# Two-layer decode attention and MLP with all gradients on one core: softmax by halves, joined layer norms, gelu by the logistic, and w1 turned in the softmax's gaps

## The chip, the core and the metric

The kernel runs on one core of one Trainium2 chip. Its time is the device time of one execution in microseconds (us). Before the change three runs gave 1210.46, 1213.57 and 1215.08 us; the median is 1213.57 us. A profile shows the engines by short names: PE is the matrix engine (PEld its weight loads), DVE the vector engine, ACT the activation engine, POOL the general engine; SP issues the loads from HBM, POOL the stores.

## What is computed

Two layers of one-token attention over a long cache, each followed by an MLP, and then the gradients of every input. Both layers use the same weights and the same cache. Batch is 2, the model width 1024, 32 query heads share 4 key/value heads of 128, the cache has 16384 positions, and the MLP is 3584 wide.

```python
def _layernorm(x, axis=-1, eps=1e-5):
    m = jnp.mean(x, axis=axis, keepdims=True)
    v = jnp.var(x, axis=axis, keepdims=True)
    return (x - m) / jnp.sqrt(v + eps)

def _A_ref(x, k_cache, v_cache, wq, wo):
    q = (x @ wq).reshape(B, Sq, Hq, Dh).transpose(0, 2, 1, 3)
    k = jnp.repeat(k_cache, rep, axis=1)
    v = jnp.repeat(v_cache, rep, axis=1)
    scores = jnp.einsum("bhqd,bhkd->bhqk", q, k) * (Dh ** -0.5)
    p = softmax(scores)
    o = jnp.einsum("bhqk,bhkd->bhqd", p, v)
    return o.transpose(0, 2, 1, 3).reshape(B, Sq, Hq * Dh) @ wo

def _B_ref(x, w1, b1, w2, b2):
    y = _layernorm(x)
    h = gelu(y @ w1 + b1)          # the tanh form
    return h @ w2 + b2

x = x + _A_ref(_layernorm(x), ...)
x = x + _B_ref(_layernorm(x), ...)
x = x + _A_ref(_layernorm(x), ...)
x = x + _B_ref(_layernorm(x), ...)
```

The outputs are the last x and the gradients of x, both caches, wq, wo, w1, b1, w2 and b2, in bfloat16. The MLP's input is normalised twice in a row, once outside and once inside `_B_ref`.

## The kernel before

**Data in time.** A group is one batch entry and one key/value head, so there are eight. Each group's K or V comes in four chunks of 1 MB (32 tiles of 128 positions). Weights come in chunks of up to 1 MB as well. Chunks live in slots: 14 in a fixed pool, and three to seven more in tiles that are unused at that time (`last`, half of `e1`, `ds1`). The class `Program` records the kernel as a list of pieces, and each piece names the chunks that it reads. `run` then walks the list, gives chunks to free slots in the order of first use, and issues each load on SP as soon as its slot's old content has had its last use. So SP loads in the order of first use, far ahead if slots are free, and waits if the next slot is still being read. The pieces are also the order of the instructions on every engine; nothing reorders them.

**Stages.** Forward attention of layer 0 (`attn_fwd(0, ...)`), MLP of layer 0, forward attention of layer 1, MLP of layer 1 forward and backward, backward attention of layer 1, MLP of layer 0 backward, backward attention of layer 0. The last stage also makes all weight and cache gradients (`kv_outputs`, `dw_units`) and stores them. Some chunks of K and V stay in their slots from the end of one stage to the start of the next (`keep0`, `keep1`).

**Forward attention.** It runs 128 steps, 16 to a group. A step turns eight K tiles on PE (L322, `ablock`), copies them out of PSUM on ACT or DVE, whichever a running balance favours (`copy_bf`, L191 and L194), and two steps later (`SKEW`) multiplies them by the queries (L636). Scores of a group fill two PSUM banks, one per half. `softmax` hangs its parts on later steps of the same count: `m0` and `m1` take maxima of the halves (L527, L532), `m2` turns them and joins them over partitions (L538 to L542), `m3` spreads the negative maximum (L547, L549), `ex` makes the exponentials, one ACT instruction for each head and half, with the maximum as a bias and the sum accumulated (L556), and `m4` adds the sums over partitions and inverts them (L566, L567). The product with V (L619) follows `LAG_F` = 24 steps behind the step that turned the matching K. Blocks of wq and wo for the next and the last head pair are spread between (L476, L495).

**Around the change.** `ln_fwd` and `ln_bwd` are generators; each `yield` marks where a sum over partitions by PE (`part_sum`, L379) is waited for, and `chain` emits other pieces at these places. `mlp_in` and `mlp_in_bwd` each run two of them in a row. `gelu_fwd` and `gelu_slope` work on tiles of 128 x 56. For layer 1 the rows of w1 are needed twice: as they are in `w1_fwd` (L656) and turned in `w1_bwd` (L693). `w1_turned` turns them (PE L349, copies L191, L194 or L352). The first two chunks are turned into two extra slots during the layer norms, the other six in place in `w1_fwd`'s loop. `wo_now` turns wo's blocks, eight pieces, between the gelu and `w1_bwd`. The backward attention's own first steps turn V tiles as the forward steps turn K.

## Time and profile before

| what | value |
|---|---|
| median of three runs | 1213.57 us |
| the profiled execution | 1217.15 us |
| its span, first to last instruction | 1215.4 us |
| mean granted PE clock | 0.841 of full speed |
| PE busy | 1049.3 us, 86% |
| DVE busy | 616.8 us, 51% |
| ACT busy | 585.2 us, 48% |
| read from HBM | 352.37 MB |
| written to HBM | 98.62 MB |

The profile is of one execution. Busy times count overlapped work on different engines separately. A wait is put down to the instruction that ended it. "Lnnn" is the line of the kernel before, as printed above, and names such as `kT<-tp` say which tile is written from which. The page divides the span into 40 slices; its digits are tenths busy:

```profile
PE   6888896688999888888889898988998899889996
...
DMA  9999999989999992999999885899999999999995
GB/s 343 379 420 421 421 421 421 368 320 357 401 419 422 418 379 103 376 420 421 418 404 351 304 345 197 310 405 362 409 418 363 378 411 420 378 397 406 416 414 203
```

Each slice is 30.4 us. DMA moves about 420 GB/s where it is full.

### The profile page before, as it was taken

Reading aid. Unit: us, or ns where it says so; the run is one execution under the profiler, and the core shown is the slowest. Engines: PE = TensorE matmul, PEld = TensorE weight load, DVE = VectorE, ACT = ScalarE, POOL = GpSimd, SP = SyncE. Lnnn points to the kernel's source line nnn. Section 1 sums busy time; section 2 is a strip of 40 time slices with the busy share of each in tenths; the row PEclk is TensorE's granted clock in tenths of the full one; section 3 lists DMA queues with packets and bytes.
Section 4 is the critical chain, followed back from the end, with each engine's and each line's share of the span. In section 5 each row is a group of like instructions: output and inputs, shape, how many; then the busy total and the mean of one; then the engine's idle time right before and its main releaser. Section 6 shows DMA issues by size and latency. Waiting matters only on the chain. (4 is left out here: it accounts for less than half of the span.)

```text
span 1215.4 us, 44602 instructions
## 1 busy us (share of the span) xinstructions
PE 1049.3 (86%) x19820; PEld 882.8 (73%) x19849; DVE 616.8 (51%) x1303; ACT 585.2 (48%) x1426; POOL 126.5 (10%) x216
## 2 busy tenths in 40 slices
PE   6888896688999888888889898988998899889996
PEld 5878896688899888888889887565565556556663
DVE  2333342234333424433333343877886787778775
ACT  1443343024433533233434332766775677667774
POOL 0000000000000000000000001322222222222222
PEclk8866675589666858789989987998998899999998
DMA  9999999989999992999999885899999999999995
GB/s 343 379 420 421 421 421 421 368 320 357 401 419 422 418 379 103 376 420 421 418 404 351 304 345 197 310 405 362 409 418 363 378 411 420 378 397 406 416 414 203
DMA packets 106045, 453.87 MB, mean 373 GB/s; under 512 B 8658, under 2 KB 8658, under 8 KB 75516
## 3 DMA queue, kind: packets, MB, share of 16 engines
q1 hardware_dynamic: 78780, 352.36, 73.7%
q0 software_dynamic: 27072, 98.66, 20.1%
q8 instruction: 155, 2.54, 0.8%
q14 instruction: 38, 0.31, 0.1%
HBM read 352.37 MB, written 98.62 MB: 371 GB/s over the span
## 5 line engine op out<-in xcount | busy, mean ns | idle before, releaser
L191 ACT COPY kT<-tp 128x512 int32<-128x512 int32 x377 | 220.7, 585 | 425.1 <-PE tp L322 351.3
L322 PE MATMUL tp<-ident,slot 128*128 128x128 bf16 x4224 | 374.4, 241 | 6.6 <-issue 3.9
L194 DVE COPY kT<-tp 128x1024 bf16<-128x1024 bf16 x259 | 178.9, 691 | 266.7 <-PE tp L322 218.3
L322 PEld LDWEIGHTS <-slot 128*128 128x128 bf16 x4224 | 289.9, 108 | 24.1 <-issue 10.0
L199 ACT CAST slot<-sc 128x512 bf16<-128x512 f32 x271 | 157.7, 589 | 51.3 <-PE sc L996 19.8
L202 DVE CAST slot<-sc 128x512 bf16<-128x512 f32 x227 | 154.4, 688 | 35.6 <-PE sc L996 16.1
L996 PE MATMUL sc<-last 128*128 128x512 bf16 x324 | 119.7, 388 | 17.2 <-ACT slot L199 5.3
L911 PEld LDWEIGHTS <-kT 128*128 128x128 bf16 x2048 | 80.7, 97 | 48.2 <-issue 31.1
L892 PEld LDWEIGHTS <-slot 128*128 128x128 bf16 x1856 | 79.0, 98 | 34.3 <-issue 10.3
L911 PE MATMUL sc<-qd,kT 128*128 128x8 bf16 x2048 | 90.6, 170 | 10.5 <-issue 10.4
L1003 POOL DMA_DIRECT2D out_dram<-slot x128 | 69.0, 539 | 280.4 <-ACT slot L199 174.8
L202 DVE CAST slot<-sb 128x512 bf16<-128x512 f32 x126 | 86.7, 688 | 18.3 <-PE sb L996 6.8
L636 PE MATMUL sc<-qd,kT 128*128 128x8 bf16 x2048 | 90.7, 172 | 0.9 <-issue 0.9
L199 ACT CAST slot<-sb 128x512 bf16<-128x512 f32 x128 | 75.4, 589 | 26.6 <-PE sb L1043 14.2
L556 ACT ACTIVATE e<-sc,negm 128x64 bf16<-128x64 f32 x256 | 75.9, 355 | 7.5 <-DVE negm L549 7.3
L636 PEld LDWEIGHTS <-kT 128*128 128x128 bf16 x2048 | 73.5, 100 | 0.2
L996 PE MATMUL sb<-last 128*128 128x512 bf16 x161 | 62.4, 387 | 6.6 <-ACT slot L199 1.6
L349 PE MATMUL tp<-ident,slot 128*128 128x128 bf16 x716 | 61.4, 244 | 5.8 <-DVE slot L194 2.0
L619 PE MATMUL sb<-e,slot 128*128 128x8 bf16 x1440 | 62.4, 176 | 3.5 <-DVE rbc L567 3.1
L556 ACT ACTIVATION_READ_ACCUMULATOR e<-sc,negm 128x1 f32 x256 | 63.6, 249 | 0.0
L1043 PE MATMUL sc<-last 128*128 128x512 bf16 x155 | 56.5, 384 | 4.6 <-DVE last L1031 3.4
L619 PEld LDWEIGHTS <-slot 128*128 128x128 bf16 x1440 | 56.8, 104 | 5.0 <-issue 3.8
(314 smaller groups left out, 1317.1 us busy)
## 6 DMA issues: line engine op xcount, KB each, us to landing
slot<-in_A_k_cache_dram SPq DMA_DIRECT2D x99, 1024.0 KB, 10.0
slot<-in_A_v_cache_dram SPq DMA_DIRECT2D x93, 1024.0 KB, 11.5
out_dram<-slot POOLq DMA_DIRECT2D x182, 512.0 KB, 10.6
slot<-in_A_wq_dram SPq DMA_DIRECT2D x30, 1024.0 KB, 9.8
slot<-in_A_wo_dram SPq DMA_DIRECT2D x22, 1024.0 KB, 11.8
slot<-in_B_w_dram SPq DMA_DIRECT2D x20, 896.0 KB, 13.7
last<-in_A_k_cache_dram SPq DMA_DIRECT2D x15, 1024.0 KB, 11.3
last<-in_A_v_cache_dram SPq DMA_DIRECT2D x11, 1024.0 KB, 16.0
```

Source lines behind the costliest of these rows:

```text
L191: S.copy(out=dst.bitcast(I32), in_=src.bitcast(I32))
L194: V.tensor_copy(out=dst, in_=src)
L199: S.copy(out=dst, in_=src)
L202: V.tensor_copy(out=dst, in_=src)
L322: PE.transpose(tp[:, j, :], t, ident[:])
L556: S.activation(out=e_of(l, g)[:, 8 * f:8 * f + 8, hh, :], in_=sc[f][:, hh, :].rearrange("p (a b) -> p a b", b=8), func=ACT.Exp, bias=h["ne ...
L619: PE.matmul(acc, lhsT=c.ap[:, ((vi % 4) * 8 + j) * 128:((vi % 4) * 8 + j + 1) * 128], rhs=e[:, vi, :, j], start=(vi == 0 and j == 0), stop ...
L636: PE.matmul(sc[t // 64][:, :, t % 64], lhsT=kT[:, j, :], rhs=qd[:, 0, g, l, :], start=True, stop=True)
L892: PE.matmul(sb[0][:, 0:8], lhsT=c.ap[:, ((vi % 4) * 8 + j) * 128:((vi % 4) * 8 + j + 1) * 128], rhs=d[:, vi, :, j], start=(vi == 0 and j = ...
L911: PE.matmul(scb[0][t // 64][:, :, t % 64], lhsT=kT[:, j, :], rhs=qd[:, 1, g, l, :], start=True, stop=True)
L996: PE.matmul(ps, lhsT=hold["blk"][:, 2 * (hc % 2) + u // 2, :], rhs=flat(qms[w][:, (u % 2) * 4:(u % 2) * 4 + 4, :]), start=True, stop=True)
L1003: GP.dma_start((dKv if w == 0 else dVv)[g, :, hc * 16:(hc + 1) * 16, :], stg.rearrange("p (t d) -> p t d", d=128))
```

## The change

Five things are changed together.

1. **Softmax.** The negative maximum is added to a whole half (128 x 512) in PSUM by DVE, and one ACT instruction takes the exponential of that half without bias or accumulation. The sum comes from the rounded exponentials: PE multiplies them by a matrix of ones into the first half's bank, DVE reduces the result over positions and inverts it. This is hung four steps later than the start of the product with V, and `LAG_F` is 22.
2. **Layer norms.** The two in a row become one, with variance term v(1 + eps) + eps squared, forward and backward.
3. **Gelu.** It is written as x times (1 - s), s the logistic value 1/(1 + exp(2cu)), and the slope uses s, 1 - s and a polynomial saved by the forward part. `gelu_out` writes h; for layer 1 it comes after the slope.
4. **w1 in layer 1.** Three chunks, not two, are turned into extra slots. Five of their twelve pieces stand in the last steps of forward attention, the other seven in the layer norm. At step 130 a piece without instructions names the four V chunks of the last group; in the order of loads they stand before w1's.
5. **First steps.** The first two turns of the next attention stage are made ahead, in the chain of `attn_in(1)`, and in those of `g3_` and `g1_`. Four of the eight pieces of `wo_now` move from before `w1_bwd` to that chain.

```diff
-LAG_F = 24
+LAG_F = 22
...
+    ones_all = const.tile([128, 128], BF16, name="ones_all")
+    V.memset(ones_all[:], 1.0)
...
+    def turns_ahead(c):
+
+        holds = [{} for _ in range(SKEW)]
+        pieces = [(turn_of(lambda i=i: [c.ap[:, (i * 8 + j) * 128:(i * 8 + j + 1) * 128] for j in range(8)], h), [c])
+                  for i, h in enumerate(holds)]
+        return pieces, (c, holds)
+
+    def ablock(tiles, use, uses, mids=(), hold=None):
...
+        if hold is None:
+            hold = {}
+            emit(turn_of(tiles, hold), uses)
...
-        V.tensor_scalar(out=vpe[:], in0=ps2, scalar1=1.0 / D, scalar2=LN_EPS, op0=ALU.mult, op1=ALU.add)
+        V.tensor_scalar(out=vpe[:], in0=ps2, scalar1=(1.0 + LN_EPS if twice else 1.0) / D,
+                        scalar2=LN_EPS * LN_EPS if twice else LN_EPS, op0=ALU.mult, op1=ALU.add)
...
+        if twice:
+            V.tensor_scalar(out=nm[:, 1, :], in0=nm[:, 1, :], scalar1=1.0 + LN_EPS, scalar2=None, op0=ALU.mult)
...
-            def ex(f, hs):
+            def less(f):
                 def fn():
-                    for hh in hs:
-                        S.activation(out=e_of(l, g)[:, 8 * f:8 * f + 8, hh, :],
-                                     in_=sc[f][:, hh, :].rearrange("p (a b) -> p a b", b=8),
-                                     func=ACT.Exp, bias=h["negm"][:, hh:hh + 1], scale=1.0,
-                                     accum_out=h["esum"][:, f, hh:hh + 1])
-                        load_of("act", 0.33)
+                    V.tensor_tensor(out=sc[f][:], in0=sc[f][:],
+                                    in1=h["negm"][:].unsqueeze(2).to_broadcast([128, 8, 64]), op=ALU.add)
+                    dve(0.7)
                 return fn
 
+            def ex(f):
+                def fn():
+                    S.activation(out=e_of(l, g)[:, 8 * f:8 * f + 8].rearrange("p a h b -> p h a b"),
+                                 in_=sc[f][:].rearrange("p h (a b) -> p h a b", b=8), func=ACT.Exp)
+                    load_of("act", 0.6)
+                return fn
+
             def m4():
-                pm3 = bank[:, 32:40]
+                ps = flat(sc[0][:])
+                e = of_group(Et[l], g)
                 for f in range(2):
-                    PE.matmul(pm3, lhsT=onesf[:], rhs=h["esum"][:, f, :], start=(f == 0), stop=(f == 1))
-                V.reciprocal(out=rbc[l][:, g, :], in_=pm3)
-                dve(0.2)
+                    PE.matmul(ps, lhsT=ones_all[:], rhs=e[:, f * 512:(f + 1) * 512], start=(f == 0), stop=(f == 1))
+                es = small.tile([128, 8], F32, name="esum")
+                V.tensor_reduce(out=es[:], in_=ps.rearrange("p (a h b) -> p h a b", h=8, b=8), axis=AX.XY, op=ALU.add)
+                V.reciprocal(out=rbc[l][:, g, :], in_=es[:])
+                dve(0.9)
...
-            at(base + 21, ex(0, range(0, 6)))
-            at(base + 22, ex(0, range(6, 8)))
-            at(base + 22, ex(1, range(0, 4)))
-            at(base + 23, ex(1, range(4, 8)))
-            at(base + LAG_F, m4)
+            at(base + 20, less(0))
+            at(base + 21, ex(0))
+            at(base + 21, less(1))
+            at(base + 22, ex(1))
+            at(base + 26, m4)
...
+                if s == 130:
+                    for c in range(4):
+                        vc[7, c] = chunk_v(order[7], c)
+                    emit(lambda: None, [vc[7, c] for c in range(4)])
+                for p in tail.get(s, ()):
+                    emit(*p)
...
+    def gelu_out(l):
+        hpre, q = saved[f"gelu{l}"][:2]
+        V.tensor_tensor(out=h_all[:, :, 2 * l:2 * l + 2], in0=q[:], in1=hpre[:], op=ALU.mult)
...
+        hpre, q, sg, pl = saved[f"gelu{l}"]
+        V.tensor_tensor(out=pl[:], in0=pl[:], in1=sg[:], op=ALU.mult)
+        V.tensor_scalar(out=pl[:], in0=pl[:], scalar1=1.0, scalar2=None, op0=ALU.add)
+        V.tensor_tensor(out=pl[:], in0=pl[:], in1=q[:], op=ALU.mult)
+        return pl
...
-        y1, r1 = yield from ln_fwd(xT[:], f"m{l}a")
-        y2, r2 = yield from ln_fwd(y1[:], f"m{l}b")
+        y, rstd = yield from ln_fwd(xT[:], f"m{l}", twice=True)
...
-        dn = yield from ln_bwd(dm[:], y2[:], r2[:], "dn")
-        dx = yield from ln_bwd(dn[:], y1[:], r1[:], "dx")
+        dx = yield from ln_bwd(dm[:], y[:], rstd[:], "dx", twice=True)
...
-    chain(lambda: mlp_in(0, xA0), 4)
+    chain(lambda: mlp_in(0, xA0), 2)
...
-    chain(lambda: attn_in(1, xM0), 2)
     aflush()
+    k_now, k_first = turns_ahead(chunk_k1(down[0], 0))
+    chain(lambda: attn_in(1, xM0), 2, k_now)
...
-    w1T = [P.chunk(), P.chunk()] + ws1[2:]
-    chain(lambda: mlp_in(1, xA1), 4, w1_turned(ws1, 0, w1T[0]) + w1_turned(ws1, 1, w1T[1]))
-    hps1 = w1_fwd(1, ws1, lambda j: w1_turned(ws1, j, w1T[j], act=False) if j >= 2 else ())
+    w1T = [P.chunk() for _ in range(3)] + ws1[3:]
+    w1_now = [p for j in range(3) for p in w1_turned(ws1, j, w1T[j], act=False)]
+    xA1 = attn_fwd(1, down, lambda: xM0, chunk_k1, chunk_v1, k_first, {130 + i: [w1_now[i]] for i in range(5)})
+    chain(lambda: mlp_in(1, xA1), 2, w1_now[5:])
+    hps1 = w1_fwd(1, ws1, lambda j: w1_turned(ws1, j, w1T[j], act=False) if j >= 3 else ())
...
-    for p in wo_now:
+    for p in wo_now[:4]:
         emit(*p)
...
-    chain(g3_, 2)
+    v_now, v_first = turns_ahead(chunk_v(up[0], 0))
+    chain(g3_, 1, wo_now[4:] + v_now)
...
-    chain(g1_, 2, wo_now)
+    v_now0, v_first0 = turns_ahead(chunk_v(down[0], 0))
+    chain(g1_, 1, wo_now + v_now0)
```

## The prediction, made before the changed kernel was run

> **What bounds the kernel now.** I began with the page's slices: the DMA row stands at 9 nearly everywhere, with dips at the changes of stage. Then I asked for busy time by stage (columns: stretch, length, busy time and instructions of PE, PEld, DVE, ACT, POOL, then granted clock, DMA share, GB/s):

> ```profile
> 0.00:200.00 200.00, 164.28 (x3457) 159.10 (x3457) 64.98 (x151) 73.17 (x291) 3.03 (x11) 0.72 1.00 403
> 200.00:234.00 34.00, 17.73 (x471) 16.48 (x471) 5.49 (x31) 5.08 (x33) 1.41 (x2) 0.50 0.95 376
> ...
> 270.00:436.00 166.00, 151.66 (x3286) 148.31 (x3284) 61.35 (x129) 70.99 (x289) 0.00 (x0) 0.72 1.00 400
> 436.00:487.00 51.00, 41.41 (x828) 39.07 (x825) 16.96 (x59) 19.30 (x60) 1.38 (x2) 0.70 0.54 206
> ...
> 500.00:645.00 145.00, 128.12 (x3028) 125.48 (x3029) 56.75 (x132) 57.39 (x99) 0.00 (x0) 0.90 1.02 415
> ...
> 762.00:1190.00 428.00, 387.07 (x5310) 250.16 (x5336) 332.19 (x575) 298.38 (x549) 109.91 (x188) 0.97 1.00 393
> ```

> The rows are forward attention of layer 0; its tail, layer norms and w1 product; forward attention of layer 1; its tail, MLP and w1's backward; backward attention of layer 1; backward attention of layer 0 with the outputs. The reader should see that the DMA engines are full (1.00 to 1.02) in the four long rows and half empty (0.54) in the fourth shown, for 51 us. Who holds them there stands in the waits of the DMA queue over that stretch:

> ```profile
> SPq L286 <- PE sb L693: 25.5, 1, 25.5
> ```

> The next K/V load sat 25.5 us until `w1_bwd` (L693) gave back a buffer. So whatever lets PE reach L693 sooner is gained, if later stages follow. To see whether PE or DMA leads before it, I set issues against uses. The first w1 load of layer 1 is issued at 412.91 and lands 18.2 us later (its row in the DMA view), at 431.1; PE first reads it at 450.93 (rows: start, length, engine, line, what, count):

> ```profile
> 412.91 8.67 SPq L291 DMA_DIRECT2D slot<-in_B_w_dram  x2
> ```

> and PE's rows around it:

> ```profile
> 436.24 0.36 PE L636 MATMUL sc<-qd,kT 128*128 128x8 bf16 x8
> ...
> 445.19 3.56 PE L619 MATMUL sb<-e,slot 128*128 128x8 bf16 x128 [0.30 <-DVE rbc L567]
> ...
> 450.93 1.87 PE L349 MATMUL tp<-ident,slot 128*128 128x128 bf16 x16
> ...
> 459.67 2.34 PE L656 MATMUL sc<-m_all,slot 128*128 128x2 bf16 x84 [1.55 <-DVE sc L652]
> ...
> 486.25 0.85 PE L693 MATMUL sb<-dh_all,last 128*128 128x2 bf16 x28
> ```

> A lead of 20 us, while in layer 0's forward stage PE waits on loads (L476 on wq 6.2 us, L495 on wo 4.7). So layer 0's forward stage is bound by DMA, and from the first w2 product on by PE. PE's own waits in layer 1's forward stage are three, nearly all softmax (who waited: total, times, longest), and one group's look like this:

> ```profile
> PE sb L566 <- ACT e L556: 9.0, 6, 2.0
> PE sb L619 <- DVE rbc L567: 2.3, 7, 0.5
> PE sb L538 <- DVE mx L533: 1.6, 2, 0.8
> ```

> ```profile
> 402.59 0.34 PE L566 MATMUL sb<-esum,onesf 128*128 128x8 f32 x2
> 404.36 0.39 PE L566 MATMUL sb<-esum,onesf 128*128 128x8 f32 x2 [1.44 <-ACT e L556]
> 405.05 0.36 PE L619 MATMUL sb<-e,slot 128*128 128x8 bf16 x8 [0.30 <-DVE rbc L567]
> ```

> The sums over partitions (L566) wait for 16 exps, then PV waits for the reciprocal. Last, the clock: the stage's mean of 0.72 is 44% at full and 56% at half speed, some 93 us at half:

> ```profile
> 381.66:398.72 17.06, 17.06 (x353) 16.95 (x349) 4.82 (x10) 4.10 (x7) 0.00 (x0) 0.50 1.02 418
> ...
> 408.96:419.20 10.24, 9.44 (x257) 9.13 (x254) 4.19 (x9) 3.63 (x7) 0.00 (x0) 1.00 1.01 420
> ```

> Without any idle time PE still stayed at half speed for 17 us; a plain step (L619, L636, L322) is 1.28 us there and 0.86 us at full.

> **The change, part by part.** Sums are against the profiled execution: 1217.15 us, its span 1215.40 and 1.75 around it. It lies 3.58 above the median, 1213.57, so I carry the difference over.

> *Layer 0's forward stage.* Eight softmaxes get shorter, worth nothing: DMA at 1.00 for 200 us hides them. Without that cover they would be worth what layer 1's are. Between 200 and 234 the DMA idles 0.05 x 34 = 1.7 us because w1 buffers come back late; the joined layer norm (one round less, 215.40 to 218.98 = 3.6 us) and the shorter exps remove that cause, but no more than 1.7 can be had, since PE then waits for loads (1.6 us for w2 at 234.12). In `attn_in(1)` two of three K transposes move under the layer norm: 2.88 us at 267.71 become one step of 0.61 to 1.01, gain 1.9. Together 3.6 (bounds 1.9 and 5).

> *Softmax in layer 1, eight groups.* Removed: PE waits 9.0 + 2.3 = 11.3 us. ACT loses 16 pairs of L556 per group,

> ```profile
> L556 ACT ACTIVATE e<-sc,negm 128x64 bf16<-128x64 f32 x256 | 75.9, 355 | 7.5 <-DVE negm L549 7.3
> ...
> L556 ACT ACTIVATION_READ_ACCUMULATOR e<-sc,negm 128x1 f32 x256 | 63.6, 249 | 0.0
> ```

> 4.5 us from first to last (439.41 to 443.95), and gains two exps of 128x512, by the nearest row (L199, a PSUM cast of that shape, 589 ns) 1.2 us. DVE gains two subtractions at 0.68 (L837, same shape, from PSUM; writing back to PSUM is shown nowhere) and a reduction at 0.69 (L527): 2.1 us per group, under 61 of 166 us busy. PE exchanges two float32 products (L566, two passes each, 0.34 + 0.39 in the fence) for two 128x512 ones (L996, 388 ns each): even, and four steps after PV has begun. New wait: PV's first block needs negation 0.17, subtraction 0.68, exp 0.59, some 0.1 between each: 1.7 us after L547, with two steps (1.71 at full clock) before it. Queued behind it on PE are this step's transposes, hence the kT copies. Bounds per group 0 and 1.2 (a DVE copy of 0.69 in front and 0.5 of ACT backlog); I take 0.3, near zero since two steps cover it: 2.4 in all. So 11.3 - 2.4 = 8.9, bounds 1.7 and 11.3.

> *The clock* may add to this: with the 1.8 us holes gone some half-speed time may go, from 0 to 93 x (1 - 0.86/1.28) = 30 us. I take 1, because a cap follows at once: in the tail PE now reads w1's first chunk when the last scores are done (L636, 436.24 + 0.36 = 436.6). That load moves ahead of two wo loads (2.5 us each at 420 GB/s) and, with the 3.6 from above, lands at 431.1 - 5.0 - 3.6 = 422.5. PE can't pass it by more than 436.6 - 422.5 = 14.1. Hence 3.6 + 8.9 + 1 = 13.5 there. SP's order changes only there and by LAG_F, which asks for each V chunk two steps sooner, no load more; POOL loses two pow operations (0.7 each) and no store is passed.

> [...]

> *From 436.6 to the first L693 after 486.25: 50.4 us.* (a) Scores to PV, 8.6 us until 445.19: the chain until the negation ends takes 2.8 (439.38), subtraction, exp and gaps 1.4, so 4.2; PE meanwhile has the rest of PV (0.9), two small products (1.0) and 36 of w1's transposes (16 took 1.87 at half speed: 4.2). I take 7.0, gain 1.6. (b) Sums as wide products, at most 0.5 lost. (c) Layer norm, 8.6 us (451.06 to 459.67): one round less, but PE must do 48 transposes in it, 5.6, plus two sums 0.9, ends 2.0: 8.5, gain 0.1. (d) w1's third chunk is turned by then and leaves `w1_fwd`'s loop: 461.87 to 464.97, gain 3.1. (e) gelu and slope: 18 DVE operations (481.01 to 485.50) become 13 of about 0.2, plus a reciprocal's extra 0.3 and an exp: 3.8; before, eight wo pieces on ACT (1.07 per two) held PE for 5.2. Gain 1.4. Sum 5.7. 84 transposes at 117 or 66 ns (16 in 1.05 at full) are 4.3 us apart; I take half, 2.1. So 7.8, bounds 4 and 12.

> At L693 the gain is 13.5 + 7.8 = 21.3. The DMA queue's supply before it ended about 467 (share 0.43 from 465 to 470); moved by 3.6 it ends at 463.4, and L693 comes at 487.2 - 21.3 = 465.9, so the hole shrinks from 20 to 2.5 us and DMA keeps up.

> *The g3 and g1 chains.* One yield instead of two, but all fills now stand before the one sum. g3: 32 wo and 16 V transposes, then one half round (494.86 to 496.96): zero, bounds 1 either way, since the four moved wo pieces and the two skipped steps cancel. g1: 739.35 to 749.98, 10.6, plus two turns of 1.0 before; after, 80 transposes 8.4, sum 0.4, half round 2.1: 10.9 against 12.6, less 0.6 if a third of the unexplained 1.83 us of issue (742.63) recurs: gain 1.1; plus 0.6 from gelu's slope. 1.7, bounds 0 and 4. Layer 0's backward stage is untouched and DMA is empty before it (share 0.01 from 750 to 761.5), so it starts earlier by what PE gained.

> Sum: 21.3 + 0 + 1.7 = 23.0. 1217.15 - 23.0 = 1194.15; on the median, 1213.57 - 23.0 = 1190.6.

> **The rivals.** *The waits only change places* (0.17): subtraction and exp delay PV as much as the exps did; for it, PV's wait is on the same chain and DVE carries it too; against, 1.3 us replaces 4.5. Then 3.6 + 5.7 + 1.7 = 11: 1202.6. *The clock wakes up too* (0.15): for it, full-speed stretches end at an exp wait; against, the 17 us row. The cap binds at 14.1, B gets its 12, the chains 4: 30, so 1183.5. *Nothing to see* (0.04): the gain is given back in the last stage, DMA-full for 428 us; against, PE there has 90% and loads wait for it: 1212. *Slower* (0.08): writing PSUM in place, and exp with a strided output, cost triple, 2.0 and 1.8 us; it decides from there on. The chain becomes 4.2 against 1.7, wait 2.5, and 5 more on DVE and ACT delays the kT copies by 2, so 4.5 for 1.4 removed: 8 x 3.1 = 25 lost, against 3.6 + 5.7 + 1.7 kept: +14, 1227. Against it: L840, a DVE product of that shape with strided operands, takes 691 ns.

> **How the numbers follow.** Main case 0.56, 1185 to 1197, at 1190.6. A difference under 0.5%, 6.1 us, can't be told from none: faster is below 1207.5. Faster 0.56 + 0.17 + 0.15 = 0.88, same 0.04, slower 0.08. The range 1180 to 1205 takes in the main case, both faster rivals and the bounds.

> **What would show it.** Right: exps near 0.6 and subtractions near 0.7 us; PE's waits for ACT in layer 1's forward stage from 9 to 2; the queue's wait for `w1_bwd` from 25.5 to under 8; the stretch from the last scores to `w1_bwd` near 43. Wrong: PE waiting on w1 in the tail by more than 2 us, PV waiting over 1 us per group, or a last stage longer than before.

## The result, and the profile after

The changed kernel takes 1209.86 us (median of 20 runs, 1200.55 to 1214.3) beside 1215.59 us for the kernel before (20 runs taken with them): a ratio of 0.9949, 95% interval 0.993 to 0.9967. That is a gain of about 6 us where 23 were predicted, and the time lies above the predicted range of 1180 to 1205. The profiled execution has a span of 1209.6 us. The same kernel measured again, on another chip, gave 1206.69 us and 0.994 (0.9911 to 0.9969), with a profiled span of 1204.6 us.

To see where the gain arose and where it went, I cut the three profiles at the same products on PE: the first and last score product of layer 1's forward attention (L636 before, L661 after), the first product of `w1_bwd` in layer 1 (L693, L724), and the first and last score product of each backward attention (L911, L937). All numbers are us; the last two columns are for the two profiles of the changed kernel.

| stretch | before | after | again | gain predicted | gain measured |
|---|---|---|---|---|---|
| start to first score product of layer 1 | 270.4 | 271.1 | 270.6 | 3.6 | -0.7, -0.2 |
| its forward attention, to the last score product | 166.0 | 158.4 | 157.4 | 9.9 | 7.6, 8.6 |
| to the first product of `w1_bwd` | 49.8 | 41.9 | 42.0 | 7.8 | 7.9, 7.8 |
| `w1_bwd` and g3's chain | 16.5 | 18.9 | 19.1 | 0 | -2.4, -2.6 |
| backward attention of layer 1 | 196.4 | 199.1 | 194.8 | 0 | -2.7, 1.6 |
| MLP backward of layer 0, g1's chain | 61.7 | 62.9 | 63.3 | 1.7 | -1.2, -1.6 |
| last stage to the end | 454.6 | 457.3 | 457.4 | 0 | -2.7, -2.8 |
| span | 1215.4 | 1209.6 | 1204.6 | 23.0 | 5.8, 10.8 |

The changed kernel's busy time over four of these stretches (columns as in the prediction's first view):

```profile
271.10:429.50 158.40, 144.31 (x3293) 138.35 (x3298) 57.66 (x126) 58.83 (x103) 0.00 (x0) 0.79 1.01 403
429.50:471.40 41.90, 35.99 (x729) 33.35 (x727) 15.91 (x50) 13.40 (x26) 0.69 (x1) 0.71 0.81 315
490.30:689.40 199.10, 176.11 (x4193) 172.25 (x4191) 76.00 (x172) 79.14 (x136) 0.00 (x0) 0.90 0.97 377
752.30:1171.70 419.40, 376.51 (x5147) 243.04 (x5172) 322.72 (x559) 290.06 (x534) 107.23 (x183) 0.97 0.98 386
```

In the first row the clock rose (0.72 before, 0.79 now); in the second the DMA engines' hole shrank (share 0.54 before, 0.81 now). The queue's longest wait for `w1_bwd`, in the waits of the DMA queue from 440 to 480, fell from 25.5 to 18.9 us:

```profile
SPq L288 <- PE sb L724: 20.5, 7, 18.9
```

The softmax's own instructions came out as costed. In the groups by line (busy, mean ns, idle before) the subtraction in PSUM takes 694 ns and the exponential of a half, with its strided output, 608:

```profile
L573 DVE TENSOR_TENSOR sc<-sc,negm 128x512 f32<-128x512 f32 x32 | 20.8, 694 | 0.5
L580 ACT ACTIVATE e<-sc 128x512 bf16<-128x512 f32 x32 | 19.2, 608 | 5.0 <-DVE sc L573 4.9
```

What is new stands in PE's waits over layer 1's forward attention. Before, the list was 9.0 us for the exps, 2.3 for the reciprocal, 1.6 for the maximum. Now it begins so:

```profile
PE tp L321 <- issue: 4.5, 3, 1.7
PE sb L644 <- issue: 2.7, 2, 1.5
PE sb L494 <- issue: 2.5, 2, 1.8
PE sb L644 <- ACT e L580: 1.6, 4, 0.6
```

The waits for the exps are down to 1.6 us, but PE now idles for "issue", that is for nothing which the profile can name. With short gaps counted it is 11.0 us in the stage, where the kernel before has 1.3. The timeline shows what such a stall looks like; it falls into the middle of eight transposes whose tiles and banks are all there:

```profile
300.24 0.27 PE L321 MATMUL tp<-ident,slot 128*128 128x128 bf16 x2
302.25 0.51 PE L321 MATMUL tp<-ident,slot 128*128 128x128 bf16 x6 [1.75 <-issue]
```

Where the stalls fall tells the cause. Counted in PE's matrix products, the eight longest of the stage end at numbers 5335, 5718, 5974, 6484, 6612, 6995, 7378 and 7506; every distance is a multiple of 127 to 128. Each product has its weight load, so that is 256 instructions. The page's list of DMA queues (packets, MB, share) has a queue that moves code:

```profile
q8 instruction: 154, 2.52, 0.8%
```

It moved 154 packets of 16 KB, and PE ran 39567 instructions (19762 products, 19805 weight loads): 257 for each packet. In the trace's packet records the packet at 299.89 to 300.96 comes just before the stall's end at 302.25. In layer 1's forward attention, where the DMA engines are full (share 1.01 after, 1.00 before), two of these packets are never much less than 6 us apart: the median distance is 6.12 us after and 6.22 before, the shortest 5.86 and 5.78. The trace of before shows distances of 3.3 to 4.7 elsewhere, where the engines' share was 0.96 or less; the trace of after has a single one of 4.1 us at a share of 1.0, in the backward stage, so full engines don't hold up every packet. Counted from the stalls, no packet of the two traces starts more than 1.1 times 256 instructions ahead of the code that it brings, not even in the last stage, where the packets are 10.2 us apart (median): in these traces PE never had much more than one piece in store.

So I formed theory F, an inference from these records: in this stage PE can't run faster than its code arrives, 256 instructions in 6.1 us. The stage has 2 x 3296 instructions, 25.75 pieces, 157 us. From 166 us the softmax could win 9, whatever waits it removed. The rivals: the stalls are PE's own (P); the share of half clock sets the stage (K, and C in one expectation); the full DMA engines set it directly (D); any lead is lost in later stages (G).

### The profile page after: what moved, and what is told of

It reads as the page before. It is cut to its first block, busy times and chain, and to the rows that moved or that the text cites. A ratio compares the mean times of both kernels' runs of the same rounds, so it can differ in the third digit from the quotient of the medians.

```text
span 1209.6 us, 44046 instructions
## 1 busy us (share of the span) xinstructions
PE 1036.5 (86%) x19762; PEld 864.8 (71%) x19805; DVE 605.5 (50%) x1266; ACT 555.2 (46%) x996; POOL 125.1 (10%) x214
## 5 line engine op out<-in xcount | busy, mean ns | idle before, releaser
L191 ACT COPY kT<-tp 128x512 int32<-128x512 int32 x427 | 250.4, 586 | 428.1 <-PE tp L321 399.9
L321 PE MATMUL tp<-ident,slot 128*128 128x128 bf16 x4224 | 368.6, 238 | 12.6 <-issue 7.1
L321 PEld LDWEIGHTS <-slot 128*128 128x128 bf16 x4224 | 284.2, 107 | 29.8 <-issue 12.8
L194 DVE COPY kT<-tp 128x1024 bf16<-128x1024 bf16 x209 | 144.5, 691 | 302.7 <-PE tp L321 257.0
L199 ACT CAST slot<-sc 128x512 bf16<-128x512 f32 x271 | 157.8, 589 | 51.7 <-PE sc L1022 18.9
L918 PEld LDWEIGHTS <-slot 128*128 128x128 bf16 x1888 | 80.5, 98 | 43.1 <-issue 18.8
L937 PEld LDWEIGHTS <-kT 128*128 128x128 bf16 x2048 | 80.8, 97 | 37.7 <-issue 20.5
L661 PE MATMUL sc<-qd,kT 128*128 128x8 bf16 x2048 | 90.7, 171 | 3.6 <-issue 3.5
L937 PE MATMUL sc<-qd,kT 128*128 128x8 bf16 x2048 | 89.9, 170 | 1.0 <-issue 0.8
L199 ACT CAST slot<-sb 128x512 bf16<-128x512 f32 x128 | 75.4, 589 | 28.6 <-PE sb L1069 16.0
L661 PEld LDWEIGHTS <-kT 128*128 128x128 bf16 x2048 | 73.2, 99 | 4.1 <-issue 3.9
L362 PE MATMUL tp<-ident,slot 128*128 128x128 bf16 x692 | 58.6, 239 | 6.9 <-issue 2.9
L644 PE MATMUL sb<-e,slot 128*128 128x8 bf16 x1280 | 56.7, 176 | 8.3 <-ACT e L580 3.5
L644 PEld LDWEIGHTS <-slot 128*128 128x128 bf16 x1280 | 50.2, 102 | 11.9 <-issue 7.6
L362 PEld LDWEIGHTS <-slot 128*128 128x128 bf16 x692 | 48.3, 108 | 12.4 <-issue 9.8
L191 ACT COPY slot<-tp 128x512 int32<-128x512 int32 (+1 forms) x52 | 29.8, 574 | 52.5 <-PE tp L362 52.1
## 6 DMA issues: line engine op xcount, KB each, us to landing
slot<-in_A_k_cache_dram SPq DMA_DIRECT2D x101, 1024.0 KB, 10.1
out_dram<-slot POOLq DMA_DIRECT2D x182, 512.0 KB, 10.5
```

Source lines behind the costliest of these rows:

```text
L191: S.copy(out=dst.bitcast(I32), in_=src.bitcast(I32))
L194: V.tensor_copy(out=dst, in_=src)
L199: S.copy(out=dst, in_=src)
L321: PE.transpose(tp[:, j, :], t, ident[:])
L362: PE.transpose(tp[:, j, :], t, ident[:])
L644: PE.matmul(acc, lhsT=c.ap[:, ((vi % 4) * 8 + j) * 128:((vi % 4) * 8 + j + 1) * 128], rhs=e[:, vi, :, j], start=(vi == 0 and j == 0), stop ...
```

## The experiments

Each kernel is told by its edit. In the first four expectations the forward stage is counted from the first use of wq, some 5 to 7 us earlier than in the table; what is measured is given by the table's marks.

### Fewer bytes in layer 1's K and V loads, before and after

```diff
+    few = [32]
     def ld_kv(src, g, c):
+        n = few[0]
         return P.chunk(lambda ap: nc.sync.dma_start(
-            ap.rearrange("p (t d) -> p t d", d=128), src[g, :, c * 32:(c + 1) * 32, :]))
+            ap[:, 0:n * 128].rearrange("p (t d) -> p t d", d=128), src[g, :, c * 32:c * 32 + n, :]))
...
+    few[0] = 8
     xA1 = attn_fwd(1, ...)
...
     attn_bwd(1, ...)
+    few[0] = 32
```

> The kernel before, with the K and V loads of layer 1's two attention stages cut to a quarter of their bytes (the last three quarters of each of these chunks keep what an earlier load left there, so layer 1's scores and sums are of other data; the instructions are the same). Theory F: PE's stalls with no releaser ('issue') come when its next 256 instructions are not loaded yet; a 16 KB piece of code arrives every 6.0 us at best while the DMA engines are full and every 3.3 to 4 us while they are not. Then in backward attention of layer 1 'issue' falls from 17.2 us to under 4 and the stage from 201 to about 186; in forward attention of layer 1, where the kernel before has only 1.3 us of it, the stage stays within 3 us of 171.6, since its waits for the exps (9.1) remain. Rival P: the stalls are PE's own or come with its instruction mix; then 17.2 and 201 stay within 2 us. Rival M (the matrix products wait for loads in a way that the records don't name): both stages shrink, forward by as much as backward in share.

> The changed kernel with the same cut (layer 1's K and V loads at a quarter of their bytes, the rest of each chunk left as an earlier load left it). Theory F: the softmax's removed waits came back as waits for code, so without full DMA engines the forward attention of layer 1 loses its 11.0 us of 'issue' (to under 3) and goes from 164.9 to about 155, so that beside the kernel before with the same cut the softmax is worth 13 to 17 us in that stage instead of 6.7; backward attention of layer 1 goes from 204 to about 187. Rival P: 11.0, 164.9 and 204 stay within 2 us. Rival C (the stage is set by the share of half clock): 'issue' may go, but the stage stays within 3 us of 164.9 unless the mean clock rises above 0.80.

Measured: 1194.15 us for the kernel before with the cut, 1161.4 for the changed one (one run each; 1215.32 is the median of before there). The two attention stages of layer 1, first of the kernel before with the cut, then of the changed one with it:

```profile
266.40:432.90 166.50, 149.66 (x3298) 146.08 (x3296) 61.67 (x130) 70.64 (x288) 0.00 (x0) 0.74 0.52 179
497.10:675.10 178.00, 166.44 (x4193) 163.72 (x4191) 76.73 (x173) 78.45 (x135) 0.00 (x0) 0.96 0.57 194
```

```profile
269.00:404.40 135.40, 128.89 (x3303) 123.95 (x3300) 57.45 (x126) 58.45 (x103) 0.00 (x0) 0.93 0.64 218
461.60:642.00 180.40, 169.89 (x4190) 167.22 (x4189) 76.23 (x172) 78.97 (x136) 0.00 (x0) 0.93 0.55 191
```

With the engines half empty (shares 0.52 and 0.64) the forward stage of the kernel before stays at 166.5 us, but that of the changed kernel falls from 158.4 to 135.4, and its "issue" from 11.0 to 2.0. The backward stage falls by 18 us in both, its "issue" from 17 to 5.5, where under 4 was expected. In neither full-load stage did PE wait for a load, so the loads' own lateness doesn't explain this (against M). P, stalls that are PE's own, falls. F's sizes were too small: 10 us were expected in the forward stage and 23 came, because the clock rose as well, from 0.79 to 0.93. Of 127 steps, 113 ran wholly at full clock (74 before the cut), in 1.02 us each instead of 1.15. The main reading, from one profile of each kernel: the softmax is worth 31 us in this stage with the engines half empty, where code packets come as close as 3.7 us, and 7.6 with full ones, where the shortest distance is 5.9. Of the 31, 20.8 are PE's busy time (149.7 to 128.9 at the higher clock), the rest waits.

### The softmax alone, and all but the softmax

Edits: the kernel before with the functions `less`, `ex`, `m4` and their places, `ones_all` and `LAG_F` = 22 of the change; and the changed kernel with those of before and `LAG_F` = 24.

> The kernel before with the new softmax alone (whole halves, subtraction in PSUM, sums as wide products, a lag of 22 steps), nothing else of the change. Theory F: forward attention of layer 1 is as in the changed kernel, 165 (+-3) with about 10 us of 'issue' and under 3 us of waits for ACT, and the stretch from the last scores to the first use of w1_bwd about 49; the time is 1206 to 1211, that is nearly all that the whole change gives. The prediction's sum: 8.9 in the stage plus 1.6 in the tail, so 1205 (on 1215.6), with no new 'issue'. Rival G (what the front gains is given back in the last stage): 1214 or more.

> The changed kernel with the old softmax (16 exps per group, sums of exps, a lag of 24 steps), everything else of the change kept. Theory F: forward attention of layer 1 is back at 171 (+-3) with under 3 us of 'issue'; the stretch to the first use of w1_bwd stays near 44 (8.1 shorter came from the joined layer norm, gelu and w1's early turns, about 1.6 of it from the softmax), 2 to 3 us of that are lost again in the chain after w1_bwd, whose four pieces of wo now stand before its sum; the time is 1210 to 1214. The prediction's sum: 23.0 less 10.5 for the softmax, 12.5 gained, so 1203. Rival G: 1214 or more.

Measured: 1206.64 us for the softmax alone, ratio 0.9936 (0.9912 to 0.996), and 1212.55 us for all the rest, 0.9983 (0.9959 to 1.0006). The softmax alone gives 8.7 us where the prediction's sum has 10.5, and can't be told apart from the whole change; the rest gives 2.8 where the sum has 12.5, and can't be told from no change. With the softmax alone the forward stage takes 159.1 us with 9.5 of "issue" and 2.0 of waits for ACT; without it 167.6 with 0.6 and 12.3. From the last score product to `w1_bwd` it is 47.7 us with the softmax alone and 45.5 with the rest alone, 2.1 and 4.3 less than before: both parts gain there. Behind it the rest loses 2.8 us in g3's chain (19.3 beside 16.5) and 1.9 in g1's (63.6 beside 61.7). Rival G isn't general, since the softmax's 7 us reach the end.

### Shorter rows in the K and V loads

Edit, on the softmax alone: 16 (then 8) consecutive positions per partition instead of 128, in loads and stores alike.

```diff
-    Kv = A_k_cache.rearrange("b h (p t) d -> (b h) p t d", p=128)
+    Kv = A_k_cache.rearrange("b h (a p t) d -> (b h) p a (t d)", p=128, t=16)
...
-            ap.rearrange("p (t d) -> p t d", d=128), src[g, :, c * 32:(c + 1) * 32, :]))
+            ap.rearrange("p (a x) -> p a x", x=2048), src[g, :, c * 2:(c + 1) * 2, :]))
```

> The kernel before with the new softmax alone (1206.6 us), and another order of the tokens in the K and V chunks: 16 consecutive tokens per partition instead of 128, so that a load's rows are 4 KB long instead of 8 KB and a store of dK or dV is one piece of 512 KB with the same 4 KB rows. Theory S (size): a 16 KB piece of PE's code waits behind packets of loads that a DMA engine has taken up, and an 8 KB packet took 0.32 us; with 4 KB packets pieces come every 5 us or less while the engines are full, 'issue' in the two attention stages of layer 1 falls from 9.5 and 15.8 us to under 6 and 10, and the time to 1190 to 1200. Rival N (only fullness counts): pieces still come every 6.0 to 6.3 us, 'issue' stays within 3 us, the time within 3 us of 1206.6. Rival L: smaller rows cost the DMA engines rate, layer 0's forward stage (bound by DMA) gets longer than 199 by 4 us or more and the time is above 1210.

> The same with 8 consecutive tokens per partition: rows of 2 KB in loads of K and V and in stores of dK and dV. Theory S: pieces of code come every 4 to 5 us, 'issue' falls to under 3 and 6 us, the forward attention of layer 1 from 159 to 145 to 150 if loads keep up, the time to 1180 to 1195. Rival N: as for 4 KB, within 3 us of 1206.6 but for the stores. Rival L: above 1212, the last stage (417 us from its first to its last score product) longer by 5 us or more because its stores have 2 KB rows.

Measured: 1215.49 us (0.997 to 1.0039 of before) and 1235.85 us (1.0121 to 1.0209). S falls: code came every 6.26 us in both (median in the forward stage), so the time of a piece doesn't hang on the size of the packets around it, and "issue" rose from 9.5 to 14.8 and 12.7 us. N had this right and the times wrong. L holds: layer 0's forward attention, which DMA bounds (share 1.00 in the profile of before), went from 184.4 us to 188.3 and 196.3 between its score products. Here rows should stay long.

### Pieces of wo before `w1_bwd`, code moved, the sum first

Three kernels around the chains. The first puts all eight pieces of wo back before `w1_bwd` (`for p in wo_now`, and `chain(g3_, 1, v_now)`). The second adds 64 transposes of the identity at the start of the changed kernel. The third is the first with a new order in `chain`:

```diff
         for i in range(gaps):
-            n = -(-len(fill) // (gaps - i))
-            for f in fill[:n]:
+            for f in fill[:gaps]:
                 emit(*f)
-            fill = fill[n:]
+            fill = fill[gaps:]
             emit(lambda: next(hold["g"], None))
+        for f in fill:
+            emit(*f)
```

> The changed kernel with all eight pieces of wo before w1_bwd, as in the kernel before (the change moved four of them behind it, into the wait for the sum). Theory F: the pieces took 4.8 us between w1_bwd and the sum (two of them 1.46 us late for code) where the chain waits for nothing, so without them the stretch from the end of w1_bwd to the first product of backward attention falls from 13.1 to 9 us while w1_bwd starts 2.3 us later; net 1 to 2.5 us, 1207.5 to 1209. Rival (the prediction's zero): the two cancel and the time stays within 1 us of 1209.9. Rival G (any lead is lost in the stages that follow): 1209 to 1211, with the lead of 2 us at the first product of backward attention gone at its last.

> The changed kernel with 64 transposes of the identity more on PE in its first microseconds (128 instructions, half a piece of code), so that every later piece of code ends half a piece earlier in the work; nothing else. Theory A (place): the last 3 us that the changed kernel loses against the softmax alone come from where its pieces of code happen to end (1.5 us between w1_bwd and the sum, 2.3 us around the last w1_bwd); the stalls then sit elsewhere, the stage from first to last product of backward attention of layer 1 moves by 2 to 5 us from 199 and the time by 2 to 5 us from 1209.9, either way. Rival B: the time stays within 1.5 us of 1209.9 and the stages within 1 us; the place of the pieces doesn't matter, only their number.

> The changed kernel with all eight pieces of wo before w1_bwd (as in the run before, 1205.7 us) and with the transposes that fill a layer norm's wait placed behind its last sum where they stood ahead of it: one piece ahead of the sum of a norm with one round, two ahead of each sum of a norm with two, all others behind the last. The data for the sum are there 0.7 us after the last product, while 64 to 80 transposes ahead of it held it until 4.1 us (g3) and 7.7 us (g1) after; behind the sum they run under the half round of 2.2 us in which PE waited. Theory F: from the end of w1_bwd to the first product of backward attention 8.1 us becomes 6.2, in layer 0 from 20.5 to 18.3, and in layer 1's mlp_in 10.1 becomes 8.8; 5 us in all, of which stages paced by code keep most: 1200 to 1203. Rival G (a lead is lost in the stages that follow): 1204.5 or more. Rival Z (the transposes' copies on DVE delay the chain by what the order saves): the three stretches stay within 0.5 us and the time within 1.5 us of 1205.7.

> The changed kernel once more, on the chip of the run before, as its measure and for a second look at its stages: forward attention of layer 1 from first to last score product within 1.5 us of 158.4, the stretch to w1_bwd within 1 us of 41.9, backward attention of layer 1 within 3 us of 199.1, the last stage's score products within 3 us of 419.4; time 1207 to 1212.

Measured: 1205.69 us (0.9901 to 0.9953 of before) for the first, 1207.68 (0.9915 to 0.9974) for the second, 1204.03 (0.9898 to 0.9952) for the third, and 1206.69 for the changed kernel again, on the third's chip. The first was faster than the 1207.5 to 1209 expected, the third slower than its 1200 to 1203, and the changed kernel's second backward stage of layer 1, 194.8 us, lies outside the 3 us around 199.1.

What the chain lost is plain in PE's timeline of the changed kernel after the last product of `w1_bwd` (start, length, engine, line, what, count, idle before):

```profile
477.25 1.33 PE L362 MATMUL tp<-ident,slot 128*128 128x128 bf16 x11
480.04 2.42 PE L362 MATMUL tp<-ident,slot 128*128 128x128 bf16 x21 [1.46 <-issue]
482.28 1.89 PE L321 MATMUL tp<-ident,slot 128*128 128x128 bf16 x16
483.96 0.53 PE L392 MATMUL sc<-lb_s,onesf 128*128 128x4 f32 x2
486.54 0.34 PE L804 MATMUL sb<-gA_all,ds 128*128 128x2 bf16 x8 [2.05 <-DVE gA_all L780]
```

The sum (L392) needs data that DVE had finished 0.7 us after the last product, and stands behind 48 transposes until 483.96; then PE idles 2.05 us with nothing left to fill. The same place with the sum first:

```profile
481.57 1.01 PE L321 MATMUL tp<-ident,slot 128*128 128x128 bf16 x8
482.39 0.59 PE L392 MATMUL sc<-lb_s,onesf 128*128 128x4 f32 x2
482.84 1.01 PE L321 MATMUL tp<-ident,slot 128*128 128x128 bf16 x8
484.96 0.35 PE L805 MATMUL sb<-gA_all,ds 128*128 128x2 bf16 x8 [1.11 <-DVE gA_all L781]
```

From the end of `w1_bwd` to the first product of backward attention it takes 13.1 us in the changed kernel, 8.1 with wo before and 7.4 with the sum first as well; g1's stretch goes from 20.9 to 18.8 and layer 1's layer norm from 10.1 to 9.3, each within 1.2 us of what was expected (Z falls). The totals follow less clearly: 1204.0 against 1206.7 on one chip, with runs of the changed kernel from 1198 to 1214, so a gain of 2 to 3 us is likely and not shown. Moving the code by half a piece (128 instructions) shifted the backward stage by 3.3 us against the first profile, but the changed kernel's own two profiles differ there by 4.3, so neither this nor the total says anything about the place of the pieces.

The stall itself does. Both profiles of the changed kernel have it after the 11th of the 32 transposes, that is after 235 products from the start of `w1_bwd`. With the code moved by half a piece it is gone from there:

```profile
477.83 3.58 PE L362 MATMUL tp<-ident,slot 128*128 128x128 bf16 x32
```

With wo before, the 32 transposes stand ahead of `w1_bwd`, and the stall comes after 203 of its 224 products, again 235 from the same point of the code (the rows of its last 28):

```profile
477.72 0.33 PE L724 MATMUL sb<-dh_all,ds 128*128 128x2 bf16 x7
479.45 0.72 PE L724 MATMUL sb<-dh_all,ds 128*128 128x2 bf16 x21 [1.41 <-issue]
```

So it sits at a place in the code and not at a place in the work, as F has it. Without it the stretch of `w1_bwd` and g3's chain takes 17.1 us instead of 18.9 and 19.1.

### Half the products, and wide products

Two cuts in the product with V, each in both kernels. First, every second tile of V is left out and the others get 128 columns; then all eight products get 128 columns.

```diff
+                    if l == 1:
+                        e2 = of_group(Et[l], vg)[:, vi // 2 * 128:vi // 2 * 128 + 128]
+                        for j in range(0, 8, 2):
+                            PE.matmul(sb[vpos % 2][:, 272:400], lhsT=..., rhs=e2, ...)
+                        return
...
-                        for j in range(0, 8, 2):
+                        for j in range(8):
```

> The changed kernel with the product of e and V in layer 1's forward attention done for every second tile of V only (four of each step's eight products left out, so layer 1's attention output is of half of V), and the other four with 128 columns of e instead of 8: a pair of weight load and product with 128 columns takes 76 ns on PE (8 in 0.61 us) and one with 8 columns 45 ns (8 in 0.36), so four of the one take 0.31 and eight of the other 0.36 us: almost the same time on PE with 1024 instructions, four pieces of code, less in the stage; all loads are as they were. Theory F: the stage loses four times 6.1 us: from 157.4 to 158.4 (two looks) to 133 to 140, or up to 148 if loads come late first, and its 'issue' falls from 11 to 12 us to under 5. Rival P (PE's own work or its clock sets the stage): 154 to 159. Rival D (the DMA engines, full in this stage, set it): 154 to 159 with new waits for DMA in place of 'issue'.

> The same cut in the kernel before (every second tile of V left out in layer 1's forward attention, the others with 128 columns). Theory F: there the waits for the exps set the stage and code came in time (1.3 us of 'issue'), so the stage stays within 6 us of 166. Rival P: it gets shorter by as much as the changed kernel's. If both shrink alike, the number of PE's instructions counts by PE's own time and not by the code's arrival.

Measured: the stage takes 144.2 us in the changed kernel, its "issue" 4.0 us, and 153.0 in the kernel before. The first fits F, with loads late at last: 6.4 us of waits for DMA in the stage, and then PE stands before w1 (waits from 269 to 430):

```profile
PE tp L362 <- DMA slot<-in_B_w_dram: 11.3, 1, 11.3
```

w1's first chunk was usable at 425.4, so that is the other cap on a lead there (the prediction put it at 422.5). The second run is a miss for F: within 6 us of 166 was expected, and it fell by 13, with the clock at 0.91 instead of 0.72. The cut had moved instructions and clock at once and told nothing apart. Hence two more runs, with the count kept:

> The changed kernel with all eight products of e and V per step in layer 1's forward attention, each with 128 columns of e instead of 8 (so layer 1's attention output holds other sums; nothing is left out). The instructions are as many as before, loads too; a pair of 128 columns takes 76 ns where one of 8 takes 45, so PE has 0.25 us more to do per step at full clock, 32 us in the stage. Theory F: 51 instructions of PE per step at 6.1 us for 256 make 1.22 us, 156 us in the stage, whatever PE does in a step as long as it does it in less; at full clock a step would be 0.86 + 0.25 = 1.11, so the stage stays between 156 and 162 if the wider products keep the clock as high as in the two runs with four of them (0.91 to 0.96). Rival P (PE's work sets the stage): 157.4 plus most of 32, 175 or more. Rival K (the stage's length is the share of half clock): with a mean clock above 0.9 the stage falls below 150.

> The same in the kernel before. Theory F: the code's pace is the same floor of 156 us, the exps' waits (9 to 12 us) come on top as far as the code hasn't caught up in them: 160 to 170, though PE has 32 us more to do than in the 166 us of before. Rival P: 185 or more. Rival K: below 155.

The forward stage of the changed kernel with wide products, then of the kernel before with them:

```profile
268.60:425.40 156.80, 150.50 (x3296) 145.36 (x3301) 57.89 (x126) 59.04 (x103) 0.00 (x0) 0.99 1.01 404
```

```profile
267.90:433.20 165.30, 152.65 (x3300) 149.36 (x3298) 62.10 (x130) 70.62 (x288) 0.00 (x0) 0.97 0.98 396
```

PE had some 32 us more to do at full clock, and the clock was 0.99 instead of 0.79, yet the stage takes 156.8 us beside 158.4 and 157.4. The kernel before with them takes 165.3, within the 160 to 170 expected. Neither PE's work alone (P, 175 or more) nor its clock alone (K, below 150) sets it, and the DMA engines don't either (D), for with the same loads it took 144.2. It is 25.75 pieces at 6.1 us, 157.

One rival is left by these two runs: more work at a higher clock could come out the same by chance, for PE was busy 150.5 of the 156.8 us. The other kernels exclude it. The softmax alone with rows of 4 KB has the same products, 8 columns wide, and its forward stage reads

```profile
277.60:434.50 156.90, 138.63 (x3294) 132.10 (x3299) 57.87 (x126) 58.76 (x103) 0.00 (x0) 0.86 1.02 395
```

From this kernel to the one with wide products PE's busy time goes from 138.6 to 150.5 us, the clock from 0.86 to 0.99 and "issue" from 14.8 to 3.6, and the stage stays at 156.9 and 156.8. All eight profiles of kernels with the new softmax, all their products, full loads and rows of 4 or 8 KB lie between 156.8 and 160.0. This settles F for the forward stage. The backward stage of layer 1 has 2 x 4192 instructions, 32.75 pieces, 200 us by the same count, and takes 193 to 200 in the kernels with full loads and rows of 4 or 8 KB; some of its packets are closer together, so the count is only an upper mark there.

## Why the prediction was wrong

**Where the missing gain lies.** The sum was 23.0 and the first profile shows 5.8. Of the 17.2 us between them 4.3 lie before layer 1's first score product, 2.3 in its forward attention, 2.4 in g3's chain, 2.7 in layer 1's backward attention, 2.9 in g1's stretch and 2.7 in the last stage, while the tail gave 0.1 more than said. So the steps that failed are the 3.6 of layer 0's forward stage, the zero for g3, the 1.7 for g1 and the zeros for layer 1's backward attention and the last stage, more than the 9.9 for the softmax and the clock. The runs with parts agree: most of what is missing is missing from the rest, not from the softmax.

**The softmax step had the right terms and lacked a limit.** "Removed: PE waits 9.0 + 2.3" came true: ACT's part went from 9.0 to 1.6, and the new wait for the exps is 0.2 us per group where 0.3 was taken. What failed is the sentence "a cap follows at once", which named w1's load, 14.1 us away, as the only cap. Code arrival caps the stage at 157 us, 9 below the 166.0 of before. Removed waits (7.4 for ACT, 2.4 for DVE) came back as 9.7 us of "issue"; the 7.6 that remain go with the clock's rise from 0.72 to 0.79, down to the pace of the code and no further. That 8.9 + 1 came near is luck. The rival "the clock wakes up too" came from a bound of 30 us on the clock's share; with fewer bytes loaded 20.8 us of busy time went, with full engines 7.4. The limit could be read in the profile of before: its backward stage has 10.4 us of idle time at L911 put down to "issue", and its code packets are 6.1 us apart there (median). I noted "issue" for one gap of 1.83 us alone and didn't ask what it was.

**Layer 0's forward stage (3.6) gave nothing, and the profile of before flatters it.** Two things cancel in the table's first row. In the profile of before the loads were slow up to 60 us (the page's slices show it: 343 and 379 GB/s, then 420):

```profile
15.00:60.00 45.00, 36.45 (x763) 35.03 (x760) 14.70 (x29) 17.06 (x54) 0.00 (x0) 0.81 1.02 377
60.00:190.00 130.00, 110.76 (x2330) 107.62 (x2328) 44.88 (x97) 51.90 (x232) 0.00 (x0) 0.67 1.02 421
```

The four other profiles with the old softmax have 419 or 420 GB/s in the first of these stretches, and layer 0's forward attention takes 179.4 to 179.8 us there between its score products, where that profile has 184.2. With the new softmax the loads are slower throughout:

```profile
60.00:190.00 130.00, 105.95 (x2245) 100.98 (x2249) 37.75 (x86) 39.35 (x69) 0.00 (x0) 0.70 1.02 413
```

The nine profiles with it and rows of 8 KB have 413 or 414 GB/s there and 182.7 to 184.4 us. So the forecast that the softmax is "worth nothing" in this stage was some 4 us too good. In the three pairs taken on one chip each (fewer bytes, half the products, wide products) the first score product of layer 1 comes 2.7, 3.2 and 0.7 us later with the change. The slower loads come with the softmax's edit, for the kernel with all the rest has 421. They don't come from its exponentials: from 5 to 15 us the loads run at 415 to 417 instead of 421 to 423, and the first exponential starts at 36 us or later. What in the edit does it no run shows.

The claim that shorter exps and the joined layer norm leave w2's start to DMA held: it moved only from 234.1 to 233.3. Removed waits became waits for loads; in layer 0's forward attention they went from 11.5 to 23.3 us while ACT's went from 12.4 to 1.6. But the 1.9 us for two turns made ahead did not show: from the last product of w1 to the first score product it took 39.9 and 39.1 us, before 38.0. In all profiles this stretch runs from 36.7 to 42.1, long where the clock was low (0.70 to 0.83), so 1.9 us can neither be seen nor excluded.

**The tail (7.8) was right**, 7.9 and 7.8: layer norm, w1's early turns, gelu. The stretch is 41.9 us where about 43 was said, its clock 0.71 beside 0.69. The runs with parts give 2.1 us of it to the softmax and 4.3 to the rest, 1.5 less than both together, so the total fits better than its parts. The wait for `w1_bwd` was to fall below 8 us and fell to 18.9 only, since PE came there 14.8 us earlier and not 21.3.

**g3's chain ("zero") lost 2.4 and 2.6.** "The four moved wo pieces and the two skipped steps cancel" missed that the pieces in front of the one sum hold it back by 6 us, 1.5 of them a stall for code, while the half round behind it has no cover. Putting the sum first brought the stretch with `w1_bwd` to 14.4 us, below the 16.5 of before, at the price of 2.2 us for the four pieces of wo ahead of it.

**g1's chain and the slope (1.7) lost 1.2 and 1.6.** The same order of fills is one part (2.1 us came back with the sum first). The rest lies within what the stretch varies: 58.3 to 65.7 us in kernels whose code there is that of before.

**Layer 1's backward attention (0) lost 2.7 and won 1.6.** The changed kernel's two profiles differ by 4.3 us, more than either gap. In the pairs on one chip the stage takes 2.4, 5.1 and 6.5 us longer with the change. It has the same instructions there and runs near the pace of its code; why it varies by that much stays open.

**The last stage (0) lost 2.7.** It takes 454.0 to 454.6 us in the five profiles with the old softmax, up to 456 in most others with rows of 8 KB, and 457 to 459 in four with the changed kernel's code. In two of these PE waits 2.5 us at the same place, in the first profile because DVE and ACT stand 2.4 and 2.0 us there for a staging buffer whose store has not landed; in the other two I found no such place. Why some kernels meet it stays open. It is not that DMA bounds the stage, as the rival "nothing to see" had it: the DMA share there fell from 1.00 to 0.98 and the stage did not shrink.

**The sign and the rivals.** Faster was right. "Slower" fell with 694 and 608 ns for the two instructions it rested on. "Nothing to see" (1212) came nearest in time; the last stage gave back 2.7 of its gain, not all. "The waits only change places" (1202.6) was right that waits come back, but for another wait than the one it named: not the subtraction and the exponential took the exps' place, but the arrival of code. Of the signs of being wrong that were named, one came: the last stage got longer.

## What to carry to other kernels

Count PE's instructions per stage, products and weight loads together, divide by the instructions for each code packet (256 here) and multiply by the distance of the code packets in that trace (6.1 us here with full DMA engines). A stage near that product gained little from removed waits here (7.6 us, where 31 came with the engines half empty), and idle time marked "issue" at distances that are multiples of 128 products was its sign. Before a stage's length is taken from one profile, compare its load rate with another's: here 45 us of slow loads in the profile of before hid a loss of some 4 us. In a chain that waits for a sum, put the sum as early as its data allow and the fill behind it: here that took g1's stretch from 20.9 to 18.8 us. Of the versions tried, the one with the sum first is the fastest, 1204.0 us or 0.9925 (0.9898 to 0.9952) of before; the softmax alone, 0.9936, and the changed kernel with wo before, 0.9927, are not told apart from it.

## What the runs showed of the hardware

In layer 1's forward attention the granted clock was higher with wide products at nearly the same busy share of PE. Eight products per step with 128 columns instead of 8 took it from 0.79 to 0.99, where PE was busy 96% of the stage (150.5 of 156.8 us) instead of 91% (144.3 of 158.4), and in the kernel before from 0.72 to 0.97, with 92% (152.7 of 165.3) instead of 91% (151.7 of 166.0). Four of them took it to 0.91 there, with PE busy 89% (135.5 of 153.0). The width isn't all that counts: with 8 columns the clock was also 0.83 in the changed kernel's second profile (busy 90%), 0.86 with rows of 4 KB (88%) and 0.93 with fewer bytes (95%). What sets it no run here shows.

Rows of 2 KB instead of 8 KB in K, V and their gradients cost the kernel 29 us (1235.9 beside 1206.6).
